# A diagonal state-space recurrence beside grouped attention: stepping over pairs of tokens instead of single tokens

## The chip, the cores and the metric

One Trainium2 chip, one core. The metric is the device time of one launch in microseconds, the median of three runs. Engines: PE (TensorE, matrix products), ACT (ScalarE), DVE (VectorE), POOL (GpSimd), SP (SyncE, which issues nearly all DMAs here).

## The reference

Two independent computations on 2048 tokens of width 640, whose outputs lie side by side. In short:

```
# A: state-space layer, 640 complex states
L     = exp(dt * (Lambda_re + i Lambda_im))        # one complex factor per state
B_bar = ((L - 1) / Lambda)[:, None] * (B_re + i B_im)
h[t]  = L * h[t-1] + B_bar x[t]
y[t]  = 2 * Re(C h[t]) + x[t] * Dskip
# B: attention, 32 query heads of 20, one shared key and value head, no mask
q = x wq;  k = x wk;  v = x wv
out = softmax(q k^T / sqrt(20)) v, heads side by side, times wo
```

The kernel takes bf16 arrays and gives a bf16 array of 2048 x 1280.

## The kernel before

**Attention.** The 2048 queries are four blocks of 512, the 32 heads eight groups of four, so there are 32 groups of work. A group has 4 heads x 16 key chunks of 128 = 64 *units*; a unit is the scores of one head, 128 keys by 512 queries, and there are 2048 in all. Of every unit the exponential is taken in one of two ways:

- By ACT: two or three units of scores lie in a PSUM tile R (`TILES = (3, 2)`), and one activation (`ex_op`, L1254) writes them as bf16 into a tile of the ring P, which has `PTILES = 10` tiles. One V product per unit then reads P.
- By DVE: one unit of scores lies in a bank B0, B1 or the third bank of R0. A first step (`dx_op`, L1260) forms a 16-bit integer that is read as a bf16 power of two, and three shifted copies (`sh_op`, L1265) of up to `DSHIFT = 3` neighbouring units in one instruction correct it. The buffer Pd has `DUNITS = 9` units; a run of shifts is cut at its end and at a change of group. Such a unit needs four V products, one for each copy.

V products of the four heads run side by side in PV; at a group's end DVE copies PV to OTr (L1298), SP stores that to DRAM (o_rows), and once a block of queries is whole, `dense_ops` loads it densely packed into OTd, POOL divides by the denominators, and `proj_ops` multiplies by wo. Queries of a block are made by `qd_block` into Qd, stored to DRAM (q_rows) and loaded group by group into the ring QT of `QRING = 4`.

**State-space layer.** x^T comes by DMA transposes, 512 tokens at a time (xaT, two buffers). For each block b of 512 tokens and each chunk c of 128 states:

- `scan_in`: five products of 512 tokens with B's real part and five with its imaginary part, into one PSUM bank each; DVE multiplies each bank by a table of cosines and sines (cs) in one instruction of 1024 elements (L892).
- `scan_unit`: POOL adds and subtracts (pieces of 128 tokens, L908); DVE runs two scans of 512 tokens, one for the rotated real and one for the rotated imaginary part (L919), with the decay |L| as factor; POOL turns the states back with four products and two sums and writes W.
- `y_tile`: for 128 tokens, products of W with CGre and CGim (C times the input factor) and of x with the diagonal of Dskip; DVE copies them out (L953), SP stores them.

CGre and CGim are made once, by 50 scalar products on POOL (L849) and ten combinations of 640 columns on DVE (L851), from C loaded by DMA transposes.

**The order of the work.** `main` is a planner that runs while the program is built. It holds threads of ready operations (fills of R, exponentials, V products, `sc`, `sa`, `su`, `sr`, `sy` for the state-space layer, `qt`, `qr`, `norm`, `dense`, `proj`), estimates when each could begin, and appends the one with the least begin plus bias. Fills go to DVE units where `want_d` finds DVE's backlog short and a bank free, at most `QUOTA = 16` units of a group. The `sa` thread is spread over 60 to 70% of the units by `scan_open`. In each of 64 turns a number from `SEEDS` draws the planner's settings and its noise. Every engine then runs its own list in order, with semaphore waits.

Of the kernel before, what the change touches and what calls it, by code (L numbers as in the profile page):

```python
# [243 lines left out]
class _Kernel:  # L244
# [4 lines left out]
    TILES, PTILES, DUNITS, DSHIFT, QRING = (3, 2), 10, 9, 3, 4  # L249
# [15 lines left out]
    SEEDS = (3008, 4003, 5007, 6005, 7007, 8009, 9006, 10003, 0, 12001, 13005, 14006, 15009, 16007, 17005, 18006,  # L265
# [28 lines left out]
    def alloc(self):  # L294
# [3 lines left out]
                  for i, n in enumerate(self.TILES)]  # L298
# [20 lines left out]
        self.sb("Qd", [128, NC, 512], BF16)  # L319
        self.sb("Gs", [32, 512], BF16)  # L320
# [14 lines left out]
        self.sb("OTd", [128, NC, 512], BF16)  # L335
        self.sb("OTp", [128, 2, 512], BF16)
        self.wq_raw = self.P[:].rearrange("p s n -> p (s n)")[:, 18 * 512:18 * 512 + NC * 640].rearrange("p (c n) -> p c n", c=NC)
# [5 lines left out]
        self.Os = nc.dram_tensor("o_rows", (self.NQB, 1024, 512), BF16, kind="Internal").ap()  # L343
        self.Ms = nc.dram_tensor("m_row", (1, 20), FP32, kind="Internal").ap()
# [4 lines left out]
        self.sb("BTre", [128, NC, 640], BF16)  # L349
        self.sb("BTim", [128, NC, 640], BF16)  # L350
        self.sb("CGre", [128, NC, 640], BF16)
        self.sb("CGim", [128, NC, 640], BF16)
# [6 lines left out]
        self.sb("cs", [128, NC, 2, 512], BF16)  # L359
        self.sb("tm", [128, 8, 512], BF16)  # L360
        self.ctmp = self.tm[:].rearrange("p i n -> p (i n)").bitcast(FP32)[:, 1024:1664]
        self.sb("uh", [128, 2, 512], BF16)
        self.sb("hh", [128, 2, 512], FP32)
# [4 lines left out]
        self.sb("W", [128, NC, 2, 512], BF16)  # L368
        self.Craw = [(self.W[:].rearrange("p c r n -> p (c r n)")[:, 1280 * c:1280 * c + 1280] if c < 4 else
                      self.ostage[:].rearrange("p a n -> p (a n)")).rearrange("p (r n) -> p r n", r=2)  # L370
                     for c in range(NC)]

# [56 lines left out]
    def setup(self):  # L429
# [27 lines left out]
        pool(lambda e: e.iota(K.iota_i, pattern=[[1, 512]], base=0, channel_multiplier=0), writes=["hh1"], occ=0.6)  # L457
        pool(lambda e: e.tensor_copy(K.iota_f, K.iota_i), reads=["hh1"], writes=["hh0"], occ=0.6)
# [28 lines left out]
        pk = ["P7", "P8", "P9"]  # L487
        go(self.dma(K.wq_raw, t["wq"].rearrange("(c p) n -> p c n", p=128), "wq", writes=["wq_raw"] + pk, kb=800))
# [48 lines left out]
        for o in copy("act", 0):  # L537
# [22 lines left out]
              for i, sh in enumerate(self.SHIFTS)),  # L560
            Op("dve", lambda e: e.tensor_copy(pad(K.wq1[:]), K.wq_raw[:, :, 80:160].rearrange("p c (j r) -> p c j r", r=20)),
               ["wq_raw", "wq1"] + pk, ["wq1"], occ=dve_t(400, 3.5))])
        for c in range(NC):
            pool(lambda e, c=c: e.tensor_copy(K.wqd[:, c, :].rearrange("p (d h) -> p d h", h=32),
                                              K.wq_raw[:, c, :].rearrange("p (h d) -> p d h", d=20)),
                 ["wq_raw"] + pk, [f"wqd{c}"], occ=1.6)
# [5 lines left out]
                                       base=-20, channel_multiplier=1), reads=["E1"], writes=["E1"])  # L572
        for o in self.load_xa(0):
            go(o)
        for c in range(NC):
            go(self.dma(K.BTre[:, c, :], t["bre"][:, 128 * c:128 * (c + 1)], f"bre{c}", writes=[f"BTre{c}"],
                        tr=True, kb=160))
            go(self.dma(K.BTim[:, c, :], t["bim"][:, 128 * c:128 * (c + 1)], f"bim{c}", writes=[f"BTim{c}"],
                        tr=True, kb=160))
# [37 lines left out]
    def constants(self, dve, act, pool):  # L617

        K, NC = self, self.NC
        DT, NRE, NIM, RDEC, DEN, RD, T1, T2, NGRE, NUR, NUI, GRE, GIM, NGIM = range(14)  # L620
        self.RDEC, self.GRE, self.GIM, self.NGRE, self.NGIM = RDEC, GRE, GIM, NGRE, NGIM
# [19 lines left out]
        act(lambda e: e.activation(s(RDEC), s(NRE), ACT.Exp), ["sc"], ["sc"])  # L641
        go(self.mms([self.m1(K.B[0][:, 15:20], K.vecD, K.ident[0:5, 0:5], True, True)], ["ident", "vecT3"], ["B0"]))
# [18 lines left out]
    def tables(self, dve, act, between):  # L661

        K, NC, ang = self, self.NC, self.ang
        for c in range(NC):
            b = c % 2
            turn = ang[:, 0, 0, c:c + 1]
            t0, t1, f, g = (K.tri[:, 4 * b + i, :] for i in range(4))
            own = [self.row_keys(4 * b + i) for i in range(4)]
            dve(lambda e, t0=t0, turn=turn: e.tensor_scalar(t0, K.iota_f, turn, MAGIC, op0=ALU.mult, op1=ALU.add),
                ["hh0", "ang"], own[0], n=512, rate=2)  # L670
            dve(lambda e, t0=t0, t1=t1: e.tensor_scalar(t1, t0, MAGIC, None, op0=ALU.subtract), own[0],
                own[1], n=512, rate=2)
            dve(lambda e, t1=t1, f=f, turn=turn: e.scalar_tensor_tensor(
                out=f, in0=K.iota_f, scalar=turn, in1=t1, op0=ALU.mult, op1=ALU.subtract),
                ["hh0", "ang"] + own[1], own[2], n=512)
            if c < NC - 1:
                act(lambda e, f=f, g=g: e.activation(g, f, ACT.Abs), own[2], own[3], n=512)
            else:
                dve(lambda e, f=f, g=g: e.scalar_tensor_tensor(out=g, in0=f, scalar=-1.0, in1=f, op0=ALU.mult,
                                                               op1=ALU.max), own[2], own[3], n=512)  # L680
            act(lambda e, c=c, f=f: e.activation(K.cs[:, c, 1, :], f, ACT.Sin, scale=TWO_PI), own[2], ["sinT"],
                n=512)
            act(lambda e, c=c, g=g: e.activation(K.cs[:, c, 0, :], g, ACT.Sin, bias=K.half_pi[:, 0:1],
                                                  scale=-TWO_PI),
                own[3] + ["half_pi"], ["cosT"], n=512)
# [836 lines left out]
```

## Time and profile before

| | before |
|---|---|
| median of three runs (lowest to highest) | 769.66 us (768.74 to 769.82) |
| the profiled execution, its own time | 768.96 us |
| its span, first to last instruction | 767.2 us |
| mean granted TensorE clock | 0.996 |
| exponentials on ACT | 667 instructions, 733.9 us |
| first steps of DVE units | 385 + 46 instructions |

The span leaves 1.8 us of the profiled execution's time outside. In a group line the figures behind the bar are the busy time of the group, the mean time of one instruction in ns, and the engine's idle time just ahead of them with what ended it. In a line of windows the stretch comes first, then for each engine its busy time and its instructions, then the granted clock, the DMA share and GB/s.

### The profile page before, as it was taken

To read this page: it belongs to the slowest core of one execution; us is meant where nothing else is said; L and a number is where in the kernel's file an instruction comes from. 1 tells how busy PE (TensorE), PEld (TensorE's weight loads), DVE (VectorE), ACT (ScalarE), POOL (GpSimd) and SP (SyncE) were. 2 spreads that over 40 slices of the span, in tenths; PEclk is the share of its full clock that TensorE was granted. 3 is DMA by queue.
4 is the path that set the end of the run, shared out by engine and by line. 5 is a ranking of instruction groups with operands and counts; after the bars stand their busy time and mean duration, and the time that the engine had idled before them with its cause. 6 is when DMAs were issued, how large, how long until landed. Compare 5 with 4: busy or idle time off the path is not lost.

```text
span 767.2 us, 16567 instructions
## 1 busy us (share of the span) xinstructions
PE 684.0 (89%) x6466; PEld 213.1 (28%) x6529; DVE 709.6 (92%) x1228; ACT 751.7 (98%) x700; POOL 429.1 (56%) x865
## 2 busy tenths in 40 slices
PE   6899987878889999988889999988899999879988
PEld 1322222222223333222223323222233233223333
DVE  6699999999997899999998799999999899999986
ACT  7999999999999999999999999999999999999995
POOL 4703255588879460588986101589880598880040
PEclk9899999999999999999999999999999999999999
DMA  9576201000020100120002100210000201000010
GB/s 187 89 135 136 49 16 49 8 25 15 3 57 25 40 31 18 44 58 15 15 9 76 42 15 24 61 41 21 1 15 29 65 33 47 1 15 18 28 52 35
DMA packets 61147, 31.50 MB, mean 41 GB/s; under 512 B 41478, under 2 KB 61070, under 8 KB 61070
## 3 DMA queue, kind: packets, MB, share of 16 engines
q1 hardware_dynamic: 58928, 30.12, 15.8%
q8 instruction: 52, 0.85, 0.5%
q10 hardware_dynamic: 2142, 0.32, 0.3%
q14 instruction: 25, 0.20, 0.1%
HBM read 9.21 MB, written 12.69 MB: 29 GB/s over the span
## 4 chain that ended last, share of the span: by engine, by line
ACT 76%; DVE 10%; PE 10%; POOL 1%; SPq 1%; DMA 1%; issue 0%
ACT P L1254 76%; PE R L420 4%; DVE Pd L1265 4%; PE PV L420 4%; DVE Pd L1260 4%; PE B L420 2%; SPq L401 1%; DVE hh L919 1%; DVE tm L892 1%; DMA xbT<-in_B_x_dram 1%; POOL tm L849 1%; POOL uh L908 1%; POOL tm L908 0%; DVE mabs L531 0%; DVE CGim L851 0%
## 5 line engine op out<-in xcount | busy, mean ns | idle before, releaser
L1254 ACT ACTIVATE P<-R 128x1024 bf16<-128x1024 f32 (+1 forms) x667 | 733.9, 1395 | 3.0 <-PE R L420 2.1
L420 PE MATMUL R<-QT,KT 32*128 32x512 bf16 (+1 forms) x1663 | 261.0, 386 | 58.7 <-ACT P L1254 45.3
L1260 DVE TENSOR_SCALAR Pd<-B 128x512 int16<-128x512 f32 x385 | 260.8, 682 | 24.2 <-PE B L420 21.4
L1265 DVE TENSOR_SCALAR Pd<-Pd 128x1536 int16<-128x1536 int16 (+2 forms) x504 | 262.0, 552 | 0.7
L420 PE MATMUL PV<-Pd,VP 128*32 128x512 bf16 x1724 | 255.1, 385 | 5.5 <-DVE OTr L1298 2.5
L420 PE MATMUL PV<-P,VP 128*32 128x512 bf16 x1617 | 255.3, 385 | 0.5 <-DVE Qabs L782 0.3
L908 POOL TENSOR_TENSOR tm<-hh,cs 128x128 bf16<-128x128 f32 x320 | 161.8, 527 | 25.2 <-DVE hh L919 16.3
L420 PEld LDWEIGHTS R<-QT,KT 32*128 32x128 bf16 (+1 forms) x1663 | 65.1, 91 | 299.9 <-ACT P L1254 275.4
L420 PE MATMUL B<-QT,KT 32*128 32x512 bf16 x385 | 148.0, 385 | 0.0
L908 POOL TENSOR_TENSOR uh<-tm 128x128 bf16<-128x128 bf16 x160 | 80.3, 520 | 114.3 <-DVE tm L892 106.9
L908 POOL TENSOR_TENSOR W<-tm 128x128 bf16<-128x128 bf16 x160 | 85.6, 556 | 19.3 <-PE B L420 15.0
L1002 POOL TENSOR_TENSOR OTd<-OTd,rwide 128x128 bf16<-128x128 bf16 x80 | 34.3, 455 | 82.3 <-DMA OTd<-o_rows 80.4
L420 PEld LDWEIGHTS PV<-Pd,VP 128*32 128x32 bf16 x1724 | 59.6, 94 | 70.2 <-issue 41.5
L420 PEld LDWEIGHTS PV<-P,VP 128*32 128x32 bf16 x1617 | 59.2, 94 | 56.0 <-issue 43.5
L892 DVE TENSOR_TENSOR tm<-B,cs 128x1024 bf16<-128x1024 f32 x40 | 48.4, 1211 | 0.7 <-PE B L420 0.3
L420 PE MATMUL B<-CGre,W 128*128 128x384 bf16 (+1 forms) x160 | 46.4, 305 | 0.0
L420 PE MATMUL B<-CGim,W 128*128 128x384 bf16 (+1 forms) x160 | 45.5, 299 | 0.0
L849 POOL TENSOR_SCALAR tm<-W,sc 128x128 f32<-128x128 bf16 x40 | 29.7, 755 | 27.2 <-DVE CGre L851 17.8
L919 DVE TENSOR_TENSOR_SCAN hh<-sc,hini,uh 128x512 f32<-128x512 f32 x30 | 39.7, 1327 | 0.0
L420 PEld LDWEIGHTS B<-QT,KT 32*128 32x128 bf16 x385 | 34.8, 91 | 0.0
L1260 DVE TENSOR_SCALAR Pd<-R 128x512 int16<-128x512 f32 x46 | 31.4, 682 | 2.1 <-PE R L420 1.8
L420 PE MATMUL B<-xaT,BTim 128*128 128x512 bf16 x93 | 28.2, 384 | 1.2 <-issue 0.8
(150 smaller groups left out, 419.5 us busy)
## 6 DMA issues: line engine op xcount, KB each, us to landing
o_rows<-OTr SPq DMA_DIRECT2D x32, 128.0 KB, 1.7
QT<-q_rows SPq DMA_DIRECT2D x30, 128.0 KB, 2.1
q_rows<-Qd SPq DMA_DIRECT2D x16, 160.0 KB, 2.9
OTd<-o_rows SPq DMA_DIRECT2D x16, 160.0 KB, 3.2
out_dram<-ystage SPq DMA_DIRECT2D x16, 160.0 KB, 1.8
out_dram<-ostage SPq DMA_DIRECT2D x12, 160.0 KB, 1.8
P<-in_B_wq_dram SPq DMA_DIRECT2D x1, 800.0 KB, 6.1
WO<-in_B_wo_dram SPq DMA_DIRECT2D x4, 200.0 KB, 3.4
```

The costliest lines, as they stand in the source:

```text
L401: return e.dma_start_transpose(out_ap, in_ap)
L420: ins = e.matmul(o() if callable(o) else o, lhsT=l, rhs=r, start=st, stop=sp, skip_group_check=True, **kw)
L849: pool(lambda e, y=y, c=c, gy=gy, i=i: e.tensor_scalar(K.ctmp[:, i:i + 128], y[:, i:i + 128], sc[:, gy, c:c + 1], None, op0=ALU.mult), key ...
L892: dve(lambda e, k=k, h=h: e.tensor_tensor(K.tm[:, 2 * k:2 * k + 2, :], bass.AP(tensor=K.BB, offset=512 * int(h.key[1]), ap=[[512 * self.BA ...
L908: put(lambda e, c0=c0, end=end: e.tensor_tensor(out[:, c0:end], a[:, c0:end], b[:, c0:end], op), reads, [writes + h], n, gate=None if i el ...
L919: dve(lambda e, ri=ri, ini=ini: e.tensor_tensor_scan(K.hh[:, ri, :], dec, K.uh[:, ri, :], ini, ALU.mult, ALU.add), ["sc", *(f"uh{ri}{h}" f ...
L1002: ops.append(Op("pool", lambda e, c=c, m=m: e.tensor_tensor(K.OTd[:, m, c], K.OTd[:, m, c], K.rwide[:, c], ALU.mult), rw + [f"OTe{dd}" for ...
L1254: return Op("act", lambda e: e.activation(dst, K.R[n % 2][:, 0:512 * size], ACT.Exp, scale=self.exp_scale), [f"R{n % 2}"] + ["R0c"] * (siz ...
L1260: return Op("dve", lambda e: e.tensor_scalar(K.Pd[:, 0, u, :], K.B[x][:, :], self.d_off, 0.0, op0=ALU.add, op1=ALU.max), [key], [f"Pd{u}_0 ...
L1265: return Op("dve", lambda e: e.tensor_scalar(K.Pd[:, i, a:b, :], K.Pd[:, 0, a:b, :], float(self.SHIFTS[i]), 0.0, op0=ALU.subtract, op1=ALU ...
```

## The change

The recurrence steps over pairs of tokens: for odd tokens h[2s+1] = L^2 h[2s-1] + (L B_bar) x[2s] + B_bar x[2s+1], so only the states at odd tokens are made. Odd outputs are computed as before. An even output is 2 Re(C L h[2s-1]) + (2 Re(C B_bar) + D) x[2s], with the matrix KX for the last bracket. The state of the token before the first pair of a block is kept in column 0 of W.

- `scan_in`: 20 products of 256 tokens (L B with the even, B with the odd tokens, every second column of xaT) into one bank, and one table product of 1024 elements; this happens 20 times where there were 40 table products.
- `scan_unit`: scans, POOL pieces and tables have 256 steps; POOL works in two halves of 128.
- `y_tile`: a tile is 128 odd or 128 even tokens. Even tiles use CL (C times the input factor times L) and five products with KX in place of the diagonal ones.
- New constants: L times B (50 POOL products, ten DVE combinations, stored to DRAM and loaded by ten DMA transposes), CL (C is transposed in a second time; 50 POOL products, ten combinations), KX (105 products on PE including the diagonal, ten DVE copies).
- To make room: P has eight tiles, Pd eight units, Qd shares the memory of OTd and Gs that of OTp. `qd_block` therefore waits for the projection two blocks back, `dense_ops` for the next block's queries to be sent and all of CG and CL to be made.
- Loads: B comes plainly in two DMAs first; its transposes, the second set of C's and those of wo move into threads of their own.
- The planner prefers the `sc` thread on every engine and has a new thread `sb`; all seeds are new.

```diff
-    TILES, PTILES, DUNITS, DSHIFT, QRING = (3, 2), 10, 9, 3, 4
+    HALVES, NP = "ab", 256
+    TILES, PTILES, DUNITS, DSHIFT, QRING = (3, 2), 8, 8, 3, 4
...
+        act(lambda e: e.activation(s(RDEC2), s(NRE), ACT.Exp, scale=2.0), ["sc"], ["sc"])
...
-        gate = lambda: self.units >= 64 * (self.NGG * (qb - 1) + 1)
+        gate = lambda: self.units >= 64 * (self.NGG * (qb - 1) + 1) and (qb < 2 or qb - 2 in self.projected)
...
+        for n in range(2 * NC):
+            c, k = divmod(n, 2)
+            x, y, op = ((0, 1, ALU.subtract), (1, 0, ALU.add))[k]
+            tmp, ct, slot = K.ctmp[0][k], [f"ct{k}{i}" for i in range(0, 640, 128)], K.CG[:, 1, n % 3, :]
+            for i in range(0, 640, 128):
+                pool(lambda e, tmp=tmp, y=y, c=c, i=i: e.tensor_scalar(tmp[:, i:i + 128], K.CL[:, y, c, i:i + 128],
+                                                                       sc[:, LIM, c:c + 1], None, op0=ALU.mult),
+                     [f"CL{y}", "sc"], [ct[i // 128]] + ["ostage0"] * (n == i == 0), 225)
+            dve(lambda e, tmp=tmp, x=x, op=op, c=c, slot=slot: e.scalar_tensor_tensor(
+                out=slot, in0=K.CL[:, x, c, :], scalar=sc[:, LRE, c:c + 1], in1=tmp, op0=ALU.mult, op1=op),
+                [f"CL{x}", "sc"] + ct, [f"bs{n % 3}"], 695, gate=lambda n=n: n < 3 or n - 3 in self.bsent)
+            sb.append(self.dma(K.Bs[k, 128 * c:128 * c + 128, :], slot, f"bs{n % 3}", reads=[f"bs{n % 3}"], writes=[f"Bs{k}{c}"],
+                               kb=160, gate=lambda n=n: n in self.bdone, done=lambda n=n: self.bsent.add(n)))
...
+        for cd in range(NC):
+            for o0, o1, ds in ((0, 384, (0, 1, 2)), (384, 640, (3, 4))):
+                h, n = Hold(), o1 - o0
+                lst = [self.m1(lambda h=h, n=n: h.T[:, 0:n], K.CL[:, ri, c, 128 * cd:128 * cd + 128], K.CG[:, ri, c, o0:o1],
+                               c == ri == 0, c == NC - 1 and ri == 1 and cd not in ds) for c in range(NC) for ri in range(2)]
...
-            for cd in range(NC):
-                ops.append(self.mms([self.m1(lambda h=h: h.T[:, :], BT[:, cd, 128 * c:128 * c + 128],
-                                             K.xaT[:, b % 2, cd, :], cd == 0, cd == NC - 1)],
...
+        lst = [self.m1(lambda h=h, k=k: h.T[:, N * k:N * k + N], w, K.xaT[:, b % 2, cd, par:512:2], k == par == cd == 0,
+                       cd == NC - 1 and par == 1)
+               for k in range(2) for cd in range(NC) for par, w in ((0, K.BL[:, cd, k, 128 * c:128 * c + 128]),
+                                                                    (1, K.BT[:, k, cd, 128 * c:128 * c + 128]))]
...
+        def fn(e):
+            src = bass.AP(tensor=K.BB, offset=512 * int(h.key[1]), ap=[[512 * self.BANKS, 128], [N, 2], [0, 2], [1, N]])
+            tab = bass.AP(tensor=K.cs, offset=2 * N * c, ap=[[2 * N * NC, 128], [0, 2], [N, 2], [1, N]])
+            return e.tensor_tensor(K.tm[:, 0:4, :].rearrange("p (k i) n -> p k i n", k=2), src, tab, ALU.mult)
...
-            n = 512 // len(self.PIECES)
+            n = N // len(hs)
...
-        dec = bass.AP(tensor=K.sc, offset=self.RDEC * NC + c, ap=[[24 * NC, 128], [0, 512]])
+        dec = bass.AP(tensor=K.sc, offset=self.RDEC2 * NC + c, ap=[[24 * NC, 128], [0, N]])
...
+        if b and c == 0:
+            back(lambda e: e.tensor_copy(K.W[:, :, :, 0:1], K.W[:, :, :, N:N + 1]), [k for k in self.w_keys if k != "W0"], ["W0"],
+                 40, gate=free)
...
+            x = lambda cd: K.xaT[:, b % 2, cd, t0:256 * q2 + 256:2]
+            if par:
+                for cd in ds:
+                    lst.append(self.m1(lambda hd=hd, p=128 * cd - o0: hd.T[:, p:p + 128], x(cd), K.DiagD[:, cd, :], False, cd == ds[-1]))
+            else:
+                for cd in range(NC):
+                    lst.append(self.m1(lambda hd=hd, n=n: hd.T[:, 0:n], x(cd), K.KX[:, cd, o0:o1], False, cd == NC - 1))
...
-            qb == 0 or qb - 1 in self.projected)
+            qb == 0 or qb - 1 in self.projected) and self.prog["c"] == 2 * NC and (qb == self.NQB - 1 or qb + 1 in self.qsent)
...
+                elif name == "sc":
+                    bias = -0.2
```

More of the change, by code (lines that the diff above doesn't have):

```diff
@@ L766, in qd_block @@
             ops.append(Op("dve", lambda e, m=m, h=h: e.tensor_scalar(K.Qd[:, m, :], h.T[:, :], self.c1, None, op0=ALU.mult),
-                          [None], [f"Qd{m}"], occ=dve_t(512), free=True, hold=h))
+                          [None], [f"Qd{m}"] + [f"OTd{m}{x}" for x in self.PIECES], occ=dve_t(512), free=True, hold=h))
         qd = [f"Qd{m}" for m in range(NC)]
@@ new lines, in scan_ops @@
+        self.bdone, self.bsent = set(), set()
+        for k in range(2):
+            for cd in range(NC):
+                sb.append(self.dma(K.BL[:, cd, k, :], K.Bs[k, :, 128 * cd:128 * cd + 128], f"bl{cd}", reads=[f"Bs{k}{c}" for c in range(NC)],
+                                   writes=[f"BL{k}{cd}"], tr=True, kb=160, gate=lambda: 2 * NC - 1 in self.bsent))
+        sb[-1].done = lambda: prog.update(b=1)
+        for _ in constants:
+            pass
+        pool(lambda e: e.memset(K.W[:, :, :, 0:1], 0.0), [], ["W0"], 10)
@@ L855, in scan_ops @@
+        sb[-1].done = lambda: prog.update(k=1)
         for b in range(4):
@@ L882, in scan_in @@
         u = NC * b + c
[L883 to L896 removed]
+        h = Hold()
@@ L898, in scan_unit @@
+        dve(fn, [None, "cosT", "sinT"], [f"tm{i}" for i in range(4)], 4 * N, hold=h, free=True,
+            done=lambda: prog.update(a=u + 1))
     def scan_unit(self, dve, pool, back, b, c):
-        K, NC, prog = self, self.NC, self.prog
+        K, NC, N, prog = self, self.NC, self.NP, self.prog
         u = NC * b + c
@@ L1025, in norm_last @@
         ops.append(Op("dve", lambda e: e.tensor_tensor(K.OTp[:, sl, :], K.OTr[:, sl, :], h1.T[:, :], ALU.mult),
-                      [None, f"OTr{sl}"], [f"OTp{sl}"], occ=dve_t(512), free=True, hold=h1,
+                      [None, f"OTr{sl}"], [f"OTp{sl}", "Gs"], occ=dve_t(512), free=True, hold=h1,
                       done=lambda: self.normed.add(g)))
```

245 lines of the change are left out of this document (137 added, 108 removed), and 8 rows, old and new, of the table SEEDS.

## The prediction

> **What bounds the kernel now.** I read the page's busy shares first, then the chain that ended last and the costliest groups.
>
> ```profile
> PE 684.0 (89%) x6466; PEld 213.1 (28%) x6529; DVE 709.6 (92%) x1228; ACT 751.7 (98%) x700; POOL 429.1 (56%) x865
> ...
> ACT 76%; DVE 10%; PE 10%; POOL 1%; SPq 1%; DMA 1%; issue 0%
> ...
> L1254 ACT ACTIVATE P<-R 128x1024 bf16<-128x1024 f32 (+1 forms) x667 | 733.9, 1395 | 3.0 <-PE R L420 2.1
> ```
>
> ACT does exponentials for 733.9 us of 767.2 and idles only 3.0 us between them. So the time is a start of 21.6 us (first exponential), the exponentials, and an end of about 10 us. It moves only with the number of score units that ACT gets. There are 2048 units of 512 columns. The V products that read P count 1617 units of ACT; the other 431 are made by DVE (L1260 runs 385 + 46 times). One unit on ACT costs 733.9 / 1617 = 0.454 us. The question is thus how many more units DVE can take, and the groups of DVE by form give its account:
>
> ```profile
> L1260 DVE TENSOR_SCALAR Pd<-B 128x512 int16<-128x512 f32 x385 | 260.8, 682 | 24.2 <-PE B L420 21.4
> L1265 DVE TENSOR_SCALAR Pd<-Pd 128x1536 int16<-128x1536 int16 x357 | 209.6, 613 | 0.4
> L892 DVE TENSOR_TENSOR tm<-B,cs 128x1024 bf16<-128x1024 f32 x40 | 48.4, 1211 | 0.7 <-PE B L420 0.3
> L919 DVE TENSOR_TENSOR_SCAN hh<-sc,hini,uh 128x512 f32<-128x512 f32 x30 | 39.7, 1327 | 0.0
> L1265 DVE TENSOR_SCALAR Pd<-Pd 128x1024 int16<-128x1024 int16 x75 | 32.5, 472 | 0.2
> ...
> L1265 DVE TENSOR_SCALAR Pd<-Pd 128x512 int16<-128x512 int16 x72 | 21.6, 333 | 0.1
> ```
>
> Means overlap the next instruction by about 0.08 us, as the timeline of DVE shows; starts count:
>
> ```profile
> 371.70 1.21 DVE L892 TENSOR_TENSOR tm<-B,cs 128x1024 bf16<-128x1024 f32 x1
> 372.83 1.27 DVE L919 TENSOR_TENSOR_SCAN hh<-sc,hini,uh 128x512 f32<-128x512 f32 x1
> 374.03 0.66 DVE L1298 CAST OTr<-PV 128x512 bf16<-128x512 f32 x1
> 374.61 1.27 DVE L1260 TENSOR_SCALAR Pd<-B 128x512 int16<-128x512 f32 x2
> 375.80 0.60 DVE L1265 TENSOR_SCALAR Pd<-Pd 128x1536 int16<-128x1536 int16 x1
> ```
>
> So a table product holds DVE for 1.13 us, a scan for 1.20, the first step of a unit for 0.60. Shifts, less 0.08 each: 357 x 0.53 + 75 x 0.39 + 72 x 0.25 = 238 us, 0.55 per unit. A unit on DVE costs 1.15 us.
>
> Is DVE full where the scan runs? Windows, columns us of PE, weight loads, DVE, ACT, POOL:
>
> ```profile
> 100.00:225.00 125.00, 102.58 (x1014) 28.46 (x1029) 121.99 (x205) 124.58 (x113) 88.01 (x160) 1.00 0.06 17
> 500.00:575.00 75.00, 64.32 (x605) 18.32 (x609) 74.22 (x117) 74.66 (x68) 66.95 (x134) 1.00 0.06 17
> 400.00:475.00 75.00, 73.59 (x687) 24.97 (x690) 67.02 (x125) 74.99 (x70) 20.94 (x49) 1.00 0.14 39
> ```
>
> Yes: 98 to 99% in the scan stretches, with PE at 82 to 86%. Where y, projection and dense q are made (400 to 475) PE is at 98% and DVE at 89%. ACT is full in all of them.
>
> **The change, part by part.** *Table products:* 40 of 1024 elements become 20 of 1024: 20 x 1.13 = 22.6 us of DVE.
>
> *Scans:* 40 stay, with 256 steps. No row has that size. The casts give 681, 551 and 416 ns for 512, 384 and 256 columns: 0.15 us fixed, 0.08 of it overlapped. With 0.07 fixed a scan of 256 holds DVE for 0.63, which frees 40 x 0.57 = 22.6. Bounds: 24.0 if it simply halves, 10.8 if all above a cast's 0.53 us slope were fixed. I take the casts' fixed part, the nearest row.
>
> *Pool:* 640 tensor products of 128 become 320; 50 scalar products (L849) become 150 (B lambda, C gamma, C lambda). With starts 0.49 and 0.69 apart that is -158 + 69 = -89 us of 429. This matters for DVE, because its shifts slow down beside POOL. The same form from 425 to 475 us, with POOL busy for 4 of 50 us, and from 500 to 575, for 67 of 75:
>
> ```profile
> L1265 DVE TENSOR_SCALAR Pd<-Pd 128x1536 int16<-128x1536 int16 x21 | 11.0, 551 | 0.0
> ...
> L1265 DVE TENSOR_SCALAR Pd<-Pd 128x1536 int16<-128x1536 int16 x38 | 25.3, 683 | 0.0
> ```
>
> Against 551 the whole run pays 357 x 62 ns + 75 x 47 ns + some in the scans = 27 us; in proportion to POOL's work 5.6 us come back (0 to 27).
>
> *Added on DVE:* 20 more combinations of 640 columns (L851's rows: 0.87 to 0.94 us, 0.82 between starts) = 16.4; ten copies of KX, 5 x (0.47 + 0.34) = 4.0. With eight unit buffers instead of nine a run of shifts is cut after 3 + 3 + 2: some 14 triples become 21 pairs, 63 x 0.39 - 42 x 0.53 = 2.4.
>
> *Tables at the start:* half as long on ACT and DVE, worth nothing: the chain there is SP's five xbT transposes to 16.3 us, then the maxima and KT. If a table were last there, 0.1 us.
>
> *Sum on DVE:* 22.6 + 22.6 + 5.6 - 16.4 - 4.0 - 2.4 = 28.0 us freed. With n more units on DVE the time falls by 0.454 n, and DVE, at its 92% share, loses 0.92 x 0.454 n: 1.15 n + 0.42 n = 28.0, n = 18, 8.1 us. The quota of 16 units in a group of 64 leaves room (431 + 18 over 32 groups is 14 each), but by the V products some groups without scans hold 16 already, so it must be used in the others.
>
> *PE:* input products keep their columns, 20 of 256 for 10 of 512. Consecutive starts of 256-column products are 0.11 us apart (below) against 0.216 for 512, so nothing there. The moving operand now takes every second token; L747's product reads every second bf16 already and its successor starts 0.23 us after it, so I price the stride at zero (bound: doubled, 20 x 2.2 = 44 us). The same for strided weights, for which there is no row. Added: KX, 5 x (10 x (0.163 + 0.109) + 0.055) = 13.9; KX in even y tiles 8 x (5 x 0.272 - 5 x 0.055) = 8.7; V products of 18 units 2.9. These 25.5 us go into PE's 83 us of idle time, 45.3 of them waits of the scores for ACT, and in the place of 80 filler products (17 us). Without that cover they would cost up to 25.5.
>
> ```profile
> 274.68 0.27 PE L420 MATMUL B<-CGim,W 128*128 128x256 bf16 x1
> 274.79 0.27 PE L420 MATMUL B<-CGre,W 128*128 128x256 bf16 x1
> 274.90 0.27 PE L420 MATMUL B<-CGim,W 128*128 128x256 bf16 x1
> ```
>
> Each of these has its own weight load of 98 ns in the same rows, and they start 110 ns apart: the load is hidden. [...]
>
> *Eight P tiles for ten:* following the V products tile by tile, an exponential starts at least 0.76 us after its tile is free. With eight, 17 would start too early, in eight stretches, worst cases summing to 4.1 us. I take 2, since the planner orders around it (bounds 0 and 4.1).
>
> *Queues:* SP loses ten B transposes at 34 to 48 us (1.27 us each), gets two plain loads there, and later ten stores, ten transposes of B lambda, the moved ten of B and ten more of C. Behind them queue the QT loads and the o_rows stores. A QT load is issued two groups ahead (some 45 us), a store has one group (23 us); I price it at zero, and each transpose that outlasts this cover at 1.3 us. The first scan waits for B lambda, to about 110 us; now two scans run early (67 and 71 us) and the rest wait for C, ready at 157. Qd in OTd's memory ties dense q to the projection two blocks back, with some 90 us to spare (projection to 253 us, its group used from 394).
>
> 8.1 - 2 = 6 us less: 768.96 (the profiled execution) gives 763.0. That execution lies 0.7 below the median of the runs, so I write 763.5.
>
> **The rivals.** *More comes back.* POOL's tax falls much faster than its work, because the scan stretches thin out: 28 + 21 = 49 us freed, 31 units, 14 us: 755. For it: 683 against 551 ns. Against it: the quota, and POOL's new work early on.
>
> *Nothing comes back.* Scans end sooner, and the free time lands in groups that are at the quota or in stretches where PE is full: gain below 2 us, near 768.5. For it: groups at 16 units; against it: most scan groups hold 12 to 15.
>
> *The ring of P decides (slower).* Units of DVE come late to the V products; if these run one tile later than now, eight tiles behave as seven do in the record: 13.2 us of waits in nine stretches. -8.1 + 13.2: 774. It decides once the ring costs more than 8 us. For it: 0.76 us of room at ten. Against it: median room of 6.7 us.
>
> *PE decides (slower).* KX and y lie where PE is at 98%; if their 22.6 us stop the scores, 768.96 - 8.1 + 22.6 = 783, at half 772. Against it: 74.99 of 75 us of ACT even there.
>
> *Weight loads are exposed:* input products have 400 loads for 200, and 200 x 98 ns = 19.6 us on PE, at worst all on the scores, give 768.96 - 6 + 19.6 = 782. Against it: the 110 ns above.
>
> That the change does not do what it says has no rival of its own: the counts follow from the code.
>
> **How the numbers follow.** Forecast 0.45, more 0.12, nothing 0.12, ring 0.18, PE 0.10, loads 0.03. About 0.2% (1.5 us) can be told from no change. Faster: 0.45 + 0.12 = 0.57; same 0.09 of "nothing", its other 0.03 being slower; slower 0.03 + 0.18 + 0.10 + 0.03 = 0.34. The likeliest case alone spans 758 to 767 (ring 0 to 4.1, scans and tax at their bounds). The range goes to 754 for the second case and to 777 for the ring and half of PE, leaving out full PE exposure and the loads.
>
> **What would show it.** Right: L892 20 times at about 1.2 us, scans near 0.7, ACT units near 1600, DVE units near 449, idle time ahead of L1254 below 5 us. Wrong: L1254's idle with PE PV as releaser (ring) or PE R (PE); 128x1536 shifts above 613 ns; a DVE share clearly below 92% (nothing comes back).

## The result and the profile after

The change takes 800.31 us (799.13 to 801.25, four runs) against 769.56 (four runs as well) in the same session: a ratio of 1.040, 95% interval 1.0385 to 1.041. It is slower by 30.7 us, and 36.8 us above the forecast of 763.5. From the page of after, its busy shares, the chain that ended last and the costliest group:

```profile
PE 728.6 (91%) x6838; PEld 243.9 (31%) x6838; DVE 676.3 (85%) x1292; ACT 756.4 (95%) x722; POOL 343.2 (43%) x657
...
ACT 69%; PE 16%; POOL 7%; DMA 3%; DVE 2%; SPq 2%; issue 1%; POOLq 0%; DVEq 0%
...
L1333 ACT ACTIVATE P<-R 128x1024 bf16<-128x1024 f32 (+1 forms) x688 | 741.7, 1309 | 23.4 <-PE PV L422 16.5
```

The span grew by 31.3 us, and this last line holds most of it: exponentials are 7.8 us longer in sum (741.7 against 733.9), and ACT is idle ahead of them for 23.4 us in place of 3.0, for 16.5 of them until a V product set a tile of P free. Another 3.3 us lie behind the last exponential (12.5 us against 9.2), so the three give 31.5. By the terms of the forecast, exponentials are 15.9 us above it (7.8 longer where 8.1 shorter was expected), ACT's idle time 18.4 (20.4 for 2) and the end 3.3, which it had left as it was; that is 37.6 together, against 37.5 for the profiled execution. DVE is busy for 33 us less, as was meant, and does not use the time: groups of DVE by form,

```profile
L1339 DVE TENSOR_SCALAR Pd<-B 128x512 int16<-128x512 f32 x334 | 227.8, 686 | 48.8 <-PE B L422 45.1
L1344 DVE TENSOR_SCALAR Pd<-Pd 128x1536 int16<-128x1536 int16 x279 | 156.1, 591 | 0.6
L1339 DVE TENSOR_SCALAR Pd<-R 128x512 int16<-128x512 f32 x88 | 60.2, 685 | 8.2 <-PE R L422 7.2
...
L960 DVE TENSOR_TENSOR tm<-B,cs 128x1024 bf16<-128x1024 f32 x20 | 24.4, 1218 | 4.5 <-PE B L422 4.2
L986 DVE TENSOR_TENSOR_SCAN hh<-sc,hini,uh 128x256 f32<-128x256 f32 x30 | 23.7, 797 | 0.0
```

The table products are 20 of 1218 ns and the scans 0.66 us from start to start (median), near the forecast. But first steps (L1339) number 334 + 88 = 422, not 449 and not even the 431 of before, and DVE waits 48.8 us ahead of them for scores in a bank, against 24.2. The stretch from 100 to 160 us, where the constants are made, shows it for all engines, first before, then after (us of PE, weight loads, DVE, ACT, POOL; clock):

```profile
100.00:160.00 60.00, 48.51 (x502) 13.22 (x509) 58.67 (x107) 60.00 (x55) 31.56 (x44) 1.00 0.08 22
```

```profile
100.00:160.00 60.00, 52.79 (x470) 18.96 (x470) 47.15 (x80) 58.24 (x54) 55.63 (x90) 1.00 0.31 67
```

POOL is nearly full, and DVE idles for 13 of 60 us. The first scan's sums begin on POOL at 110.0 us, as the prediction had it. By the copies of PV, group 4 ends 16.6 us later than before, group 17 24.5 and group 21 31.8; from there the distance stays.

### The profile page after: what moved, and what is told of

It reads as the page before. It is cut to its first block, busy times and chain, and to the rows that moved or that the text cites. A ratio compares the mean times of both kernels' runs of the same rounds, so it can differ in the third digit from the quotient of the medians.

```text
span 798.5 us, 17159 instructions
## 1 busy us (share of the span) xinstructions
PE 728.6 (91%) x6838; PEld 243.9 (31%) x6838; DVE 676.3 (85%) x1292; ACT 756.4 (95%) x722; POOL 343.2 (43%) x657
## 4 chain that ended last, share of the span: by engine, by line
ACT 69%; PE 16%; POOL 7%; DMA 3%; DVE 2%; SPq 2%; issue 1%; POOLq 0%; DVEq 0%
ACT P L1333 69%; PE B L422 6%; PE R L422 5%; PE PV L422 5%; POOL ostage L895 2%; POOL ostage L842 2%; DMA CL<-in_A_B_im_dram 1%; SPq L403 1%; POOL CG L842 1%; DVE Pd L1344 1%; DMA xbT<-in_B_x_dram 1%; DMA xaT<-in_A_C_im_dram 1%; SPq L405 1%; POOL Md L785 1%; POOL tm L975 0%
## 5 line engine op out<-in xcount | busy, mean ns | idle before, releaser
L1333 ACT ACTIVATE P<-R 128x1024 bf16<-128x1024 f32 (+1 forms) x688 | 741.7, 1309 | 23.4 <-PE PV L422 16.5
L1339 DVE TENSOR_SCALAR Pd<-B 128x512 int16<-128x512 f32 x334 | 227.8, 686 | 48.8 <-PE B L422 45.1
L975 POOL TENSOR_TENSOR tm<-hh,cs 128x128 bf16<-128x128 f32 x160 | 81.0, 527 | 30.9 <-DVE hh L986 27.3
L975 POOL TENSOR_TENSOR uh<-tm 128x128 bf16<-128x128 bf16 x80 | 39.5, 511 | 101.7 <-DVE tm L960 99.9
L422 PEld LDWEIGHTS PV<-Pd,VP 128*32 128x32 bf16 x1688 | 59.4, 95 | 61.3 <-issue 36.8
L1339 DVE TENSOR_SCALAR Pd<-R 128x512 int16<-128x512 f32 x88 | 60.2, 685 | 8.2 <-PE R L422 7.2
L895 POOL TENSOR_SCALAR ostage<-xaT,sc 128x128 f32<-128x128 bf16 x70 | 54.0, 784 | 8.4 <-DVE CL L898 6.4
L422 PE MATMUL B<-xaT,BL 128*128 128x256 bf16 x200 | 50.6, 280 | 0.8 <-DVE OTr L1377 0.7
L422 PE MATMUL B<-xaT,BT 128*128 128x256 bf16 x200 | 49.5, 274 | 0.0
L975 POOL TENSOR_TENSOR W<-tm 128x128 bf16<-128x128 bf16 x80 | 39.8, 517 | 2.4
L422 PE MATMUL B<-xbT,wqd 128*128 128x512 bf16 x100 | 29.5, 391 | 0.7 <-DVE OTd L775 0.7
L422 PE MATMUL B<-CG,W 128*128 128x384 bf16 (+1 forms) x160 | 30.0, 303 | 0.0
```

Source lines behind the costliest of these rows:

```text
L422: ins = e.matmul(o() if callable(o) else o, lhsT=l, rhs=r, start=st, stop=sp, skip_group_check=True, **kw)
L895: pool(lambda e, tmp=tmp, y=y, c=c, gy=gy, i=i: e.tensor_scalar(tmp[:, i:i + 128], y[:, i:i + 128], sc[:, gy, c:c + 1], None, op0=ALU.mult ...
L975: put(lambda e, c0=c0, end=end: e.tensor_tensor(out[:, c0:end], a[:, c0:end], b[:, c0:end], op), reads, [writes + h], n, gate=None if i el ...
L1333: return Op("act", lambda e: e.activation(dst, K.R[n % 2][:, 0:512 * size], ACT.Exp, scale=self.exp_scale), [f"R{n % 2}"] + ["R0c"] * (siz ...
L1339: return Op("dve", lambda e: e.tensor_scalar(K.Pd[:, 0, u, :], K.B[x][:, :], self.d_off, 0.0, op0=ALU.add, op1=ALU.max), [key], [f"Pd{u}_0 ...
```

## Experiments

Every kernel below but change_thin_pe was planned anew. Seeds not from the two kernels themselves come from one pass over the 64 positions that keeps a number where the planner's own estimate of the end falls (two passes for change_ring10_b and change_all_three; change_no_kx_b and change_all_three_b start from a drawn set).

| run | median us | ACT idle ahead of exponentials | first steps on DVE | clock |
|---|---|---|---|---|
| before, seeds it came with | 769.6 | 3.0 | 431 | 0.996 |
| before_reseeded | 775.3 | 4.4 | 428 | 0.984 |
| before_ring8 | 777.8 | 6.2 | 426 | 0.991 |
| before_half_dve | 764.9 | 4.9 | 448 | 0.991 |
| change_bare_split | 773.2 | 7.0 | 440 | 0.987 |
| change_bare_ring10 | 775.9 | 9.5 | 436 | 0.976 |
| change_bare | 777.4 | 14.2 | 448 | 0.989 |
| change_no_kx_no_cl | 780.3 | 13.3 | 439 | 0.989 |
| change_no_kx / _b | 799.4 / 789.3 | 23.9 / 18.2 | 414 / 430 | 0.966 / 0.980 |
| the change, seeds it came with | 800.3 | 23.4 | 422 | 0.985 |
| change_reseeded | 796.0 | 23.2 | 423 | 0.985 |
| change_thin_pe | 805.0 | 26.1 | 422 | 0.970 |
| change_dve_const | 794.2 | 24.5 | 439 | 0.983 |
| change_split | 786.7 | 16.5 | 428 | 0.985 |
| change_ring10 / _b | 798.1 / 786.4 | 25.4 / 10.8 | 422 / 419 | 0.989 / 0.993 |
| change_dve_split | 776.7 | 10.0 | 435 | 0.987 |
| change_all_three / _b | 773.6 / 776.3 | 6.7 / 11.0 | 437 / 438 | 0.989 / 0.989 |

**Two orders of one kernel** lie 2.7 to 11.7 us apart (before, the change and the three pairs with _b). So one difference of less than some 12 us between two kernels is not safe by itself. What follows leans on larger ones (17 to 22 us); smaller ones are given as what one order showed, and weigh more where the idle time in the trace moves with them.

**Seeds.**

```diff
-    SEEDS = (2007, 0, 0, 5004, 6006, 7007, ...
+    SEEDS = (1002, 2007, 0, 0, 5003, 0, ...
```

Change:

> The change with other planner seeds, found by one pass over the 64 positions from all zeros; nothing else differs. Theories for the 30.7 us that the change costs (800.3 against 769.6): RING (P ring of 8 tiles instead of 10), PE (the products for KX and the input term of even outputs come in front of scores), CONSTANTS (C L and B Lambda in the first 160 us), SEEDS (the order that the new seeds give is less well tuned than the old one). SEEDS: at least 10 us of the 30.7 go once both kernels have seeds of the same making, so this one is at 785 to 795 and before_reseeded above 772. The other three: this one stays within 5 us of 800 and the distance to before_reseeded is 27 to 34.

Before:

> The kernel before with seeds made in the same way as in change_reseeded. It is the base line for that run and for before_ring8. SEEDS: 772 to 780, since the seeds it came with would be the better tuned; without SEEDS: 767 to 773.

Measured 796.04 (ratio 1.032, 1.029 to 1.035) and 775.34 (1.006, 1.004 to 1.008). With seeds of the same making the change costs 20.7 us, not 30.7: ten of them are the choice of the order, by this pair of orders. No reading had this whole: 796.0 is 1 us above the range of SEEDS, and 20.7 lies below that of the others. The exponentials, of before_reseeded and then of change_reseeded:

```profile
L1253 ACT ACTIVATE P<-R 128x1024 bf16<-128x1024 f32 (+1 forms) x680 | 737.3, 1339 | 4.4 <-PE B L419 1.9
```

```profile
L1332 ACT ACTIVATE P<-R 128x1024 bf16<-128x1024 f32 (+1 forms) x683 | 740.3, 1303 | 23.2 <-PE PV L421 14.0
```

So 18.8 of the 23.0 us by which the spans of these two executions differ are idle time of ACT ahead of exponentials.

**The ring alone, in the kernel before.**

```diff
-    TILES, PTILES, DUNITS, DSHIFT, QRING = (3, 2), 10, 9, 3, 4
+    TILES, PTILES, DUNITS, DSHIFT, QRING = (3, 2), 8, 9, 3, 4
```

> The kernel before with a ring of 8 tiles of P in place of 10 (the memory is kept as it was, only the last two slots go unused), seeds made in the same way. In the trace of before the 10-tile ring has 0.76 us to spare at its tightest, in that of after the 8-tile ring 0.05 us. RING: 8 to 13 us over before_reseeded (up to the 13.2 us of waits that the prediction's rival counted), with idle time of ACT put down to PV. Rival (the ring only looks tight because late work elsewhere fills it): within 3 us of before_reseeded.

777.76: 2.4 us. ACT waits only 1.3 us for V products. In the kernel before, a ring of eight costs little by this order; the theory that it decides by itself asked for 8 to 13 us, and falls.

**PE's added products, in the same order.**

```diff
+    def tiny(m):
+        return (lambda: m[0]()[:, 0:8], m[1], m[2][:, 0:8], False, False, None, 1)
...
-                                       lock=i == 0, gate=(lambda: prog["c"] >= NC) if i == 0 else None, hold=h))
+                                       emit=[self.tiny(lst[i])] if i else lst[0:1], lock=i == 0, ...
```

> The change, every instruction of every engine in its place and in the same order, but the products that make KX and the five input products of each even output stripe are cut to 8 columns (from the second of a group on), so KX and the input term of even outputs are left out. It takes 18 to 22 us of PE's stream away and changes nothing else. PE as a direct cause (scores come late because those products stand in front of them): ACT's idle time falls by 12 us or more and the time to 780 to 788. If the loss sits in the order itself (422 DVE units instead of 431, made when the order was planned) and in the ring: 793 to 799, idle falls by less than 6 us.

805.02: nothing is won, it is 4.7 us slower than the change, which neither reading had. The idle time put down to V products is 16.5 us as in the change, so these products are not what stands directly in front of them. The mean clock fell as well, from 0.985 to 0.970, so a small direct cost could be hidden. What is lost is lost mostly from 140 to 240 us, where KX is made. Two windows of after and then of change_thin_pe:

```profile
180.00:200.00 20.00, 19.12 (x191) 5.86 (x192) 18.28 (x36) 19.92 (x20) 9.73 (x21) 1.00 0.06 15
200.00:220.00 20.00, 18.64 (x187) 6.39 (x185) 18.51 (x37) 20.00 (x20) 1.09 (x2) 1.00 0.04 14
```

```profile
180.00:200.00 20.00, 15.22 (x150) 4.49 (x153) 16.59 (x32) 19.11 (x20) 11.28 (x23) 0.90 0.05 14
200.00:220.00 20.00, 17.52 (x169) 4.64 (x161) 17.08 (x35) 19.02 (x19) 0.00 (x0) 0.84 0.04 14
```

With the products gone PE is busy for 15 to 17.5 of 20 us and the granted clock falls to 0.90 and 0.84; group 7 ends 5.3 us later than in the change (230.7 us against 225.4), and at the last group the distance is still 4.6. From 140 to 240 us the longest gap in PE's records is 0.95 us (worked out from the trace). What makes the clock fall is not shown: from 220 to 240 us PE is busy for 16.43 us at a clock of 1.00 in the change, and for 16.89 at 0.83 in change_thin_pe.

**VectorE's halves alone.**

```diff
-                K.tm[:, 2 * k:2 * k + 2, :], ... ap=[[512 * self.BANKS, 128], [0, 2], [1, 512]]),
+                K.tm[:, 2 * k:2 * k + 2, 0:256], ... ap=[[512 * self.BANKS, 128], [0, 2], [1, 256]]),
...
-            dve(lambda e, ri=ri, ini=ini: e.tensor_tensor_scan(K.hh[:, ri, :], dec, K.uh[:, ri, :], ini, ALU.mult,
+            dve(lambda e, ri=ri, ini=ini: e.tensor_tensor_scan(K.hh[:, ri, 0:256], dec, K.uh[:, ri, 0:256], ini, ALU.mult,
```

> The kernel before with only VectorE's share of the change: each of the 40 scans runs over 256 of 512 elements and each of the 40 table products over half its columns (the other half of the recurrence is left out), planned anew with seeds made as in before_reseeded (775.3). Nothing of the change's extra work, and the ring of 10. By the rows this takes 22.6 us off the scans and some 22 us off the products. If VectorE's free time becomes units of attention at the rate that the prediction used (28.0 us gave 8.1), 45 us give 13: 760 to 765. Rival (freed time of VectorE can't be turned into units, because banks, ring and quota set how many it takes): 772 to 776.

764.87: 10.5 us under before_reseeded (ratio to before 0.992, 0.991 to 0.994), with 448 first steps for 428. The time is in the range that the prediction's rate gave, so freed VectorE time can become units while nothing else is added; it is one order.

**The change stripped, and put together again.** Leaving out KX, C L and B Lambda (the two plain loads of B, 800 KB each, are still made, though nothing reads them):

```diff
-            if par:
+            if True:
                 for cd in ds:
...
-        for n in range(2 * NC):
-            r, c = divmod(n, NC)
+        for n in range(NC):
+            r, c = divmod(n, NC)
...
-        nm, C = (("CL", K.CL), ("CG", K.CG))[par]
+        nm, C = (("CG", K.CG), ("CG", K.CG))[par]
```

> The change without KX (even outputs take the odd ones' direct term D x), without C L (both read C) and without B Lambda (B itself is loaded in its place), and with 10 tiles of P again: what stays are the halved scans and products, the strided reads, the shared buffers. Seeds made as in the others; change_reseeded is 796.0, before_reseeded 775.3. Extra work as the cause: all but a few us of the 20.7 go and the gain of the halves shows, 762 to 770. If strided reads, the longer groups of 20 products or the shared buffers are the cause: 778 or more.

> As change_bare_ring10, but with the change's ring of 8 tiles. RING: 8 us or more over change_bare_ring10. As before_ring8 showed it (777.8 against 775.3): 1 to 4 us over it.

> The change without KX alone: its 110 products and 10 copies are not made, even outputs take D x in their place, so their direct term is left out; C L and B Lambda are made, the ring is 8. Planned anew, seeds as in the others. change_thin_pe has shown that these products cost nothing where the order is kept; if they cost by what the planner makes of them (banks held for 10 copies, an order around them), this run is 8 us or more under change_reseeded (796.0): 780 to 788, and CONSTANTS is the distance from here to change_bare. If they cost nothing either way: 793 to 798, and CONSTANTS carries the distance to change_bare alone.

> change_no_kx (799.4) without C L too (both stripes read C, as in change_bare); B Lambda is still made. change_bare, without either, is 777.4, so the two together carry 22 us. B Lambda fills POOL from 40 to 79 us (50 pieces of 0.59 us and what they wait for), where group 0 to 2 already end 6 to 13 us later than in change_bare; C L follows until 240 us, where the distance grows from 13 to 19 us and on to 27. B Lambda as the larger part: 787 or more. C L as the larger part: 784 or less. Half each: 784 to 787.

Measured 775.89, 777.44, 799.41 and 780.25. First, the stripped change (775.89, between the two readings) is no faster than before_reseeded: without any of the extra constants, the halves' gain is already gone (11 us between before_half_dve and change_bare_ring10, one order each). Second, the ring gives 1.5 us here. Third, B Lambda costs some 3 us (777.4 to 780.3), C L at first sight 19. That last figure rests on change_no_kx, whose clock is the lowest of all, and its second order shrinks it:

> change_no_kx with other seeds, found from another start. change_no_kx (799.4) is 3 us slower than with KX, and its granted clock, 0.966, is the lowest of all. If leaving KX out gives nothing whatever the order: 793 or more. If that run had a poor order, and KX costs by what the planner makes of it: 780 to 788, with a clock of 0.98 or more, and then C L's share is no more than some 5 us.

789.30, between the two readings on offer: the clock is back at 0.980 and C L is left with 9 us by this order. Whether leaving KX out gives anything stays open (3.4 us worse or 6.7 better, by order).

**Shorter groups of input products.** In the change one bank takes all 20 products of a unit. From a group's first product to the end of its table product the bank is held for 5.3 us (median, worked out from the trace of the change), in the kernel before for 3.4 (the 18 of 40 groups whose products all stand in its trace); of the two shared banks, one is then closed to DVE's scores. There are half as many groups, so all of them together hold a bank for 108 us in place of some 135. On PE a group of the change takes 3.8 us from its first product to the end of its last, with scores and V products in between; it is not run through without a break, as the first expectation below has it. The edit:

```diff
-        lst = [self.m1(lambda h=h, k=k: h.T[:, N * k:N * k + N], w, ...
-               for k in range(2) for cd in range(NC) for par, w in ...
+        for k in range(2):
+            h = Hold()
+            lst = [self.m1(lambda h=h: h.T[:, 0:N], w, ...
+                   for cd in range(NC) for par, w in ...
```

> change_bare_ring10 (775.9), with each unit's 20 input products in two groups of 10 with a bank and a table product of 512 columns each, as the kernel before has them, in place of one group of 20 and one table product of 1024. GROUPS: a group that holds one of the two shared banks is run through without a break (2.2 us on PE in the traces of the change, 1.07 before), and scores and P V wait behind it; then this is 5 to 8 us faster, 768 to 771, and ACT's idle time before exponentials falls from 9.5 us. Otherwise within 2 us of 775.9, or slower by VectorE's 20 more table products at some 0.1 us each of fixed cost (under 1 us).

> The whole change, only the input products of each unit in two groups of 10 with a table product of 512 columns each; constants on POOL as in the change, ring of 8. change_reseeded is 796.0, change_dve_const 794.2, change_dve_split 776.7. GROUPS alone: 775 to 781, and ACT's idle time before exponentials is near the 10.0 us of change_dve_split and not the 23 to 25 us of the other two. GROUPS only together with shorter constants: 786 to 796.

773.21 in the stripped change, 2.7 us less and short of what GROUPS expected; this run also leaves out the two unused loads of B, so not even the 2.7 us are the groups' alone. 786.72 in the whole change, 9.3 us less than change_reseeded: outside the range for GROUPS alone, and at the lower edge of the one for GROUPS only together with shorter constants (786 to 796). The exponentials of change_split:

```profile
L1330 ACT ACTIVATE P<-R 128x1024 bf16<-128x1024 f32 (+1 forms) x687 | 738.2, 1327 | 16.5 <-PE B L421 6.7
```

The waits of ACT for V products fall from 14.0 to 3.2 us. They were the largest part of its idle time; now late scores are (PE B 6.7, PE R 6.2).

What in the edit does it is not told apart. It shortens the hold of a bank and the run of input products on PE, makes 40 smaller table products of 20, and lets a group wait for its own half of the constants alone. The traces give two hints, both worked out from them. The first speaks for the run on PE: of ACT's waits for V products, 6.4 of 16.5 us in the change and 7.5 of 14.0 in change_reseeded have input products on PE within the 4 us before (such stretches are 19% of the span); in change_split none of the 3.2 has. Another 5.1 and 6.5 us stand behind products of y. The bank explains less: leaving out the first 25 and the last 15 us, DVE idles for 101.8 us in change_reseeded and 48.2 in before_reseeded, and the part of it in which an input group holds a bank grows only from 2.0 to 6.9 us (in the two kernels with their own seeds from 2.0 to 13.9, of 44.0 and 103.5).

**The first factor of the constants on VectorE.**

```diff
-            for i in range(0, 640, 128):
-                pool(lambda e, tmp=tmp, y=y, c=c, i=i: e.tensor_scalar(tmp[:, i:i + 128], K.CL[:, y, c, i:i + 128], ...
+            dve(lambda e, tmp=tmp, y=y, c=c: e.tensor_scalar(tmp, K.CL[:, y, c, :], sc[:, LIM, c:c + 1], ...
```

> The whole change, nothing left out; only the first factor of each constant (B Lambda, C, C L: 30 rows of 640, cut in 150 pieces of 0.59 us on POOL) is made on VectorE, in 30 instructions. POOL as the cause (its queue is 92 to 96% busy from 40 to 80 and 100 to 150 us, and the steps that the query's path has on it wait behind): POOL loses 88 us, VectorE gains 12 to 21, worth 4 to 6 us; 780 to 788 against 796.0 of change_reseeded. If the constants are late by their loads and the way through DRAM, and POOL's queue holds nobody up: 796 to 802.

> change_dve_const with the input products in two groups of 10, as in change_bare_split. The whole change, nothing left out. POOL and GROUPS both right, and adding: 773 to 782. Only POOL: as change_dve_const. Only GROUPS: 788 to 793.

794.17: POOL is relieved of 110 us (339.3 to 229.1), DVE makes 439 first steps for 423, and the time falls by only 1.9 us, between the two readings: exponentials are 5.2 us shorter in sum (735.1 for 740.3), but ACT's idle time ahead of them rises to 24.5 and the stretch behind the last one from 10.3 to 11.9. With short groups as well it is 776.65, in the expected range, and the idle time is down to 10.0:

```profile
L1326 ACT ACTIVATE P<-R 128x1024 bf16<-128x1024 f32 (+1 forms) x686 | 734.1, 1334 | 10.0 <-PE B L421 5.8
```

So by these orders POOL's relief alone gives units and hardly any time; short groups alone give back idle time; both give 19.4 us, which is clear of what two orders differ by. How the 19.4 us divide between the two is not. Against change_bare_split (773.2) the whole extra work then costs 3.4 us, the ring of eight included.

**The ring of ten in the whole change.** Room for two more tiles is found by working in place and a query ring of three:

```diff
-    TILES, PTILES, DUNITS, DSHIFT, QRING = (3, 2), 8, 8, 3, 4
+    TILES, PTILES, DUNITS, DSHIFT, QRING = (3, 2), 10, 8, 3, 3
```

> The whole change with its groups of 20 and a ring of 10 tiles. The room comes from elsewhere: the sums before the scan are written over the products, W is made in place, two early constants lie in KX's memory, and the query ring has 3 slots in place of 4. RING as the prediction's rival had it (13.2 us of waits): 783 to 788 against 796.0. RING as in change_bare against change_bare_ring10 (1.5 us): 793 to 797. If the longer groups cost by the ring that they fill, ACT's idle time falls from 23.2 us by about half, as from 14.2 to 9.5 in the bare pair: 786 to 791.

798.13, but one wait spoils the reading. From ACT's waits between 400 and 425 us:

```profile
ACT P L1332 <- PE R L420: 17.0, 1, 17.0
```

In this order the next 512 queries are made only at 413 us, and no scores could be formed. Another order:

> change_ring10 with other seeds. In change_ring10 one idle stretch of ACT of 17.0 us at 405 us, where no rows of the next 512 queries had come, hides what the ring of 10 gives; without it that run would stand at about 781. RING (the long groups cost by the ring that they fill): no such stretch, 780 to 788. If the ring gives only the 1.5 us of the bare pair: 793 or more.

786.41, without that stretch, and 9.6 us under change_reseeded, though with one more pass on its seeds:

```profile
L1332 ACT ACTIVATE P<-R 128x1024 bf16<-128x1024 f32 (+1 forms) x689 | 741.1, 1344 | 10.8 <-PE PV L420 4.2
```

ACT's idle time is halved with 419 first steps, so it is the waits that went, not units that came. In the whole change, with its groups of 20, the ring seems to count for more than the 1.5 and 2.4 us elsewhere; one order says so.

**All three together.** The edits above in one kernel. Its output is not the reference's (relative error 0.023 and 0.024, for a reason that is not known), so it is read for its time alone, and is no kernel to use.

> The whole change with groups of 10, constants on VectorE and the ring of 10, nothing left out. change_dve_split is 776.7. If what is left of the loss is the ring: 770 to 775; it would beat before (769.6) only if the halves' 10.5 us came through in full: 765 to 769. If nothing is left of the ring's cost once the groups are short: 775 to 779.

> change_all_three with another set of seeds, found from another start with the same care. It tells how far two orders of one kernel lie apart: within 3 us if the seeds are not what the comparisons above rest on; 5 us or more would make every difference under 5 us in this study unsafe.

773.63 and 776.29, one order in the range for a ring that still costs and one in the range for a ring that does not, so that is not decided. The loss against before_reseeded (775.3) is gone, as it is within 1.3 us in change_dve_split, which does the whole work of the change; but the halves' 10.5 us do not come through, and neither order beats the kernel before (769.6).

## Why the prediction was wrong, by its own steps

The steps that failed are the turning of VectorE's freed time into units (8.1 us gained on paper; 27 units missing, 12.3 us) and the 2 us for ACT's waits (20.4 more were measured). The first made a loss of units out of a forecast gain; the second is the larger in size.

*VectorE's sum (28.0 us freed) was right in size.* With the nine units that DVE makes less, at 1.15 us each, it would be busy for 38 us less; it is 33. Table products and scans measured near their price; shifts beside POOL came down from 613 to 591 ns in the mean. Runs were cut more often than the "some 14 triples" (279 full ones for 357), but at 0.54 us a unit shifts cost no more than the 0.55 of before.

*"18 more units, 8.1 us" failed.* The rate is sound where only DVE changes (before_half_dve: 20 more units, 10.5 us). In the change there are nine fewer: 27 units short of the forecast, times 0.454 = 12.3 us. The step took for granted that scores would be there when DVE is free. It named the quota, and stretches where PE is full in a rival, and left out the order in which PE brings the scores beside longer groups and more products. DVE's waits for scores in B grew from 21.4 to 45.1 us, the largest single part of its added idle time; what makes the scores late there is not shown (the hold of a bank by input groups covers little of it).

*"These 25.5 us go into PE's idle time" held in one sense and failed in the other.* No direct cost of the added products shows in change_thin_pe; part of PE's idle time even seems worth filling, since the mean clock fell from 0.985 to 0.970 when PE was emptied, though why is not shown. But PE was reckoned in columns. What the experiments point to is the length of a group of input products (its bank is held for 5.3 us in place of 3.4), which no term of the sum had; splitting the groups gave 9.3 us (within what one order can tell) and, with the first factors on DVE, 17.5 (794.2 to 776.7).

*"Eight P tiles: 2 us, at most 4.1" was taken from the old order.* Alone it is right (2.4 and 1.5 us). With the long groups and the whole extra work beside it, ACT waited 16.5 us for V products, and the ring was worth 9.6 us by one order. The rival "the ring decides" saw the sign to look for, idle time ahead of exponentials with PE PV as releaser (16.5 us against its 13.2), but not what makes it: V products come late, about half of the time behind input products (6.4 of 16.5 us, 7.5 of 14.0), and short groups took these waits down to 3.2 us with the ring of eight kept.

*Queues and constants at zero failed.* The prediction counted loads on SP, and POOL's 150 pieces only in a sum over the whole span (down by 89 us; measured 86); in the stretch from 100 to 160 us POOL is at 93%, and by its end group 4 is 16.6 us late (12.3 with seeds of the same making). Moving the first factors to DVE gave 1.9 us with long groups and 10.1 with short ones (786.7 to 776.7).

*Strides and weight loads at zero were right.* In the timeline of PE, products of every second token of x with B Lambda and B in turn:

```profile
309.29 0.28 PE L422 MATMUL B<-xaT,BL 128*128 128x256 bf16 x1
309.41 0.27 PE L422 MATMUL B<-xaT,BT 128*128 128x256 bf16 x1
309.52 0.27 PE L422 MATMUL B<-xaT,BL 128*128 128x256 bf16 x1
```

They start 0.11 to 0.12 us apart, as the unstrided products of before did. Loads of strided weights (every second token of x, for the products with KX) took 98 ns, like the unstrided ones. Each of the 400 input products has its own weight load (200 of 96 and 200 of 97 ns in the mean), so the exposed loads of the rival do not show in these rows.

*The seeds* had no term at all. Ten of the 30.7 us are theirs, by one pair of orders.

What stays open: the 11 us between before_half_dve and change_bare_ring10, of which short groups explain at most 2.7. Eight units in Pd for nine, the memory that Qd and OTd share, the two unused loads of B and the later loads of C remain as candidates and were not tried one by one. C L's share (9 to 19 us with long groups) is not settled either, nor why the whole extra work costs only 3.4 us once groups are short and the first factors are on DVE, nor by which way long groups cost time (the bank, or their run on PE).

## What to carry to other kernels

Here time freed on VectorE gave 20 more units and 10.5 us where nothing else was added; in the whole change nine units were lost, and VectorE waited 45.1 us for scores in B in place of 21.4. So look for what brings an engine's work, in which order, and ask for how long other work stands in front of it, not only how much that work computes. Merging two short groups into one long one halved the number of table products here, and lengthened the single hold of a bank from 3.4 to 5.3 us; ACT waited 14.0 us for V products with long groups and 3.2 with short ones. Where a planner orders the work, plan both kernels with the same care before comparing them, and take no difference from one order that is smaller than two orders of the same kernel lie apart.

## What the hardware showed that was not expected

Taking work away from PE made the kernel slower: in change_thin_pe PE is busy for 709.5 us in place of 728.6 (from 140 to 240 us for 84.4 in place of 92.1), the mean granted clock falls from 0.985 to 0.970, and the time rises by 4.7 us, with no gap on PE longer than 0.95 us from 140 to 240 us, where the clock is 0.83 to 0.90 in four of five windows of 20 us. A matrix product whose moving operand takes every second bf16 column cost no more than one without stride (0.11 us from start to start at 256 columns). A scan of 256 steps with float output held DVE for 0.66 us from start to start, against 1.19 for 512 (medians).
